# Decode attention with a gated MLP on one core: another order of TensorE's last thirty microseconds, and the last block of wo in three transfers

## The chip, the cores and the metric

The kernel runs on one core of a Trainium2 chip. The metric is the device time of one execution in microseconds (us), lower is better. Beside the time of each execution the profiler gives a span, from the first to the last instruction; the time of the same execution is some 1.9 us more. Engines are named as in the profile: PE (TensorE) multiplies matrices, DVE (VectorE) and ACT (ScalarE) work on rows, POOL (GpSimd) only prepares constants here, and SP (SyncE) issues nearly all loads, strictly in the order of its program. All engines work side by side and wait for each other by semaphores.

## The reference, cut to what matters

```python
# x [4,1,640], k_cache and v_cache [4,32,8192,192], wq [640,6144], wo [6144,640], all bf16
W = 2048                                             # max(256, 8192 // 4): the last 2048 positions
xn = _layernorm(x)
q = (xn @ wq).reshape(4, 1, 32, 192).transpose(0, 2, 1, 3)
k, v = k_cache[:, :, -W:, :], v_cache[:, :, -W:, :]
p = softmax(einsum("bhqd,bhkd->bhqk", q, k) * 192 ** -0.5)
o = einsum("bhqk,bhkd->bhqd", p, v)
attn = o.transpose(0, 2, 1, 3).reshape(4, 1, 6144) @ wo
mlp = (silu(xn @ w1) * (xn @ w3)) @ w2
out = x + attn + mlp
```

There are 4 batches, 32 heads of 192, one query each, and 32 heads of keys and values. Each head's window of K is 3 MB over the four batches, and so is its window of V; together with the weights 223 MB are read.

## The kernel before, in words

The 128 partitions hold 32 groups of positions for each of the 4 batches, so one head's K or V is one tile of 128 partitions by 64 positions by 192. There are two tiles for K (`kt`) and two for V (`vt`), used by even and odd heads in turn. The setup (layernorm, q, the MLP) lies at the start of the kernel and is not touched. Below, K31 is head 31's K, V29 is head 29's V, and so on.

For each head h:

- DVE multiplies K by q in two halves (`mult(h, 0)` and `mult(h, 1)`, L272 to L277) into the two halves of `prs`.
- PE adds up six parts of each product by an identity matrix into `ps` (`adder(0)` and `adder(1)`, L420 to L427, matmuls at L373), and DVE sums the rest into the scores `sc` (`reduce_half`, L279).
- The maximum: DVE takes each partition's maximum (`chain_lmax`, L286), PE turns it into a row (`tr`, L431), DVE takes each batch's maximum from that row (`chain_gmax`, L290), ACT scales it (`gneg`, L352), PE hands it back to all partitions (`bc`, L435), ACT copies it (`negm`, L354) and takes the exponential with its row sums (L356).
- DVE spreads the exponential over the batches (`chain_z`, L295), and PE multiplies by V (`pv`, L448) into `o_ps`, which has a single buffer.
- ACT copies `o_ps` to `o_sb` (L359), and PE gathers it for a pair of heads into `po` (`osum`, L456). `tot` (L440) gathers the pair's row sums; DVE takes the reciprocal (`norm_rec`, L299), scales `po` (`norm_og`, L304) and, at every second pair, transposes four heads' o into `oT` (L307).

PE's order is written out by hand. Heads 1 to 29's steps run in a loop of 14 turns; the last two heads and the products with wo stand behind it (L491 to L531). `proj(g)` multiplies four heads' o, group g, by their block of wo: six columns of two matmuls each, 12 matmuls, all adding into `acc` (L385). Wo 0 to 4 are loaded early into the MLP's weight tiles; wo 5 to 7 at the very end into `kt[0]`, when head 30 no longer needs it. An operation waits only for its own semaphores, but on each engine everything behind it waits with it.

Before the change, PE's order from head 30 on is, with the semaphores that each waits for left out: K30's two halves around the maximum of head 29 and o of head 28; `tot`; wo 0; V29; K31's first half; the transpose of head 30's lmax; o of head 29; bc of head 30; K31's second half; V30; wo 1; the transpose of head 31's lmax; wo 2; bc of head 31; o of head 30; wo 3 and 4; `tot`; V31 in two halves; o of head 31; wo 5, 6, 7.

The ends of the loads on SP, in order: K30, K31, V29, V30, V31's first half, V31's second half, wo 5, wo 6, wo 7's first five columns, wo 7's last column. `load_v(h)` waits until the products with V of head h - 2 are done (`s_pv`, L164), because they share a tile; for head 31 this wait stands ahead of its first half only. Wo 5 waits for a count of `s_red`, which head 30's scores bring. Loads behind a waiting load on SP are not issued either.

On ACT, each head's copy of `o_ps` (L358, L359) stands behind its exponential and ahead of the next head's `gneg`. On DVE, the odd heads' `norm_rec` waits for `s_pv` so that the pair's row sums are complete; `s_tot` is raised only by the last `tot`.

At the end DVE copies `acc` to `res` (L335), and SP and ACT each send half of it out (L201, L361).

Of the kernel before, what the change touches and what calls it, by code (L numbers as in the profile page):

```python
# [16 lines left out]
def kernel(  # L17
# [15 lines left out]
    B, Sq, D = A_x.shape  # L33
    _, H, Sk, Dh = A_k_cache.shape
# [16 lines left out]
    RPP = QW // P  # L51
# [19 lines left out]
    def sb(name, shape, dt):  # L71
        return ctx.enter_context(nc.sbuf_tensor(name, shape, dt))

    def psum(name, shape, dt):
        return ctx.enter_context(nc.psum_tensor(name, shape, dt))
# [31 lines left out]
    o_sb = [sb(f"o_sb{i}", [P, 2 * Dh], FP32) for i in range(2)]  # L107
# [6 lines left out]
    o_ps = psum("o_ps", [P, QC], FP32)  # L114
# [4 lines left out]
    def sem(name):  # L119
        return ctx.enter_context(nc.semaphore(name))  # L120

    first = sem("s_first")
    (s_x, s_wq0, s_wq1, s_wq2, s_w1, s_w3, s_w2, s_k0, s_k1, s_v31, s_wom, s_wo5, s_wo6, s_wo7a, s_wo7b,
     s_gp, s_dv, s_ac, s_pp, s_ps, s_red, s_tr, s_gmax, s_bc, s_negm, s_exp, s_pv, s_sum, s_rec, s_og, s_oT,
     s_tot, s_acc) = [sem(n) for n in (
        "s_x", "s_wq0", "s_wq1", "s_wq2", "s_w1", "s_w3", "s_w2", "s_k0", "s_k1", "s_v31", "s_wom", "s_wo5",
        "s_wo6", "s_wo7a", "s_wo7b", "s_gp", "s_dv", "s_ac", "s_pp", "s_ps", "s_red", "s_tr", "s_gmax", "s_bc",
        "s_negm", "s_exp", "s_pv", "s_sum", "s_rec", "s_og", "s_oT", "s_tot", "s_acc")]
    last = sem("s_last")
    s_pr, s_lmax, s_gneg, s_z, s_v0, s_v1, s_osb, s_fin, s_out0, s_out1 = [sem(n) for n in (  # L130
        "s_pr", "s_lmax", "s_gneg", "s_z", "s_v0", "s_v1", "s_osb", "s_fin", "s_out0", "s_out1")]
# [3 lines left out]
    def take(e, s, n=1):  # L135
        e.wait_ge(s, n).then_inc(s, -n)  # L136
# [8 lines left out]
    def wo_of(hg):  # L145
        t = wts[hg // 2][:, :] if hg < 5 else wo_end
        i = hg % 2 if hg < 5 else hg - 5
        return t[:, i * RPP * D:(i + 1) * RPP * D]

    def wo_src(hg):  # L150
        return A_wo[hg * QW:(hg + 1) * QW, :].rearrange("(p i) n -> p (i n)", i=RPP)


    sp = nc.sync
# [25 lines left out]
    for h in range(H - 2):  # L180
# [3 lines left out]
        if h in (4, 6, 8):  # L184
            g = h - 4
# [3 lines left out]
                         in_=A_wo[g * QW:(g + n) * QW, :].rearrange("(g p i) n -> p g (i n)", g=n, i=RPP)).then_inc(s_wom, 16)  # L189
# [4 lines left out]
    sp.wait_ge(s_red, 2 * (H - 2) + 1)  # L194
    for hg, s in ((5, s_wo5), (6, s_wo6)):
        sp.dma_start(out=wo_of(hg), in_=wo_src(hg)).then_inc(s, 16)
    WC = RPP - 1
    sp.dma_start(out=wo_of(7)[:, 0:WC * D], in_=wo_src(7)[:, 0:WC * D]).then_inc(s_wo7a, 16)
    sp.dma_start(out=wo_of(7)[:, WC * D:], in_=wo_src(7)[:, WC * D:]).then_inc(s_wo7b, 16)
    sp.wait_ge(s_fin, 1)  # L200
    sp.dma_start(out=out_v[:, 0:N0], in_=res[0:B, :]).then_inc(s_out0, 16)  # L201
    take(sp, s_fin)
# [25 lines left out]
    ve = nc.vector  # L228
# [43 lines left out]
    def mult(h, a):  # L272
        if a == 0:
            ve.wait_ge(s_k[h % 2], 16 * (h // 2 + 1))
        ve.tensor_tensor(out=prs[:, a].rearrange("p q j d -> p (q j) d"), in0=kt[h % 2][:, 2 * a * JQ:2 * (a + 1) * JQ, :],  # L275
                         in1=qbc[:, h * Dh:(h + 1) * Dh].unsqueeze(1).to_broadcast([P, 2 * JQ, Dh]),
                         op=ALU.mult).then_inc(s_pr, 1)  # L277

    def reduce_half(h, a):  # L279
        ve.wait_ge(s_ps, 2 * h + a + 1)  # L280
        ve.tensor_reduce(out=sc[h % 3][:, 2 * a * JQ:2 * (a + 1) * JQ], in_=ps[:, a].rearrange("p q (j d) -> p (q j) d", d=DD),  # L281
                         axis=AX.X, op=ALU.add).then_inc(s_red, 1)

    def chain_lmax(h):
        ve.wait_ge(s_red, 2 * (h + 1))
        ve.tensor_reduce(out=lmax[h % 2][:], in_=sc[h % 3][:], axis=AX.X, op=ALU.max).then_inc(s_lmax, 1)  # L286

    def chain_gmax(h):
        ve.wait_ge(s_tr, h + 1)
        ve.tensor_reduce(out=gmax[h % 2][:], in_=mt[0:1, 0:P].rearrange("o (p b) -> o b p", b=B), axis=AX.X,  # L290
                         op=ALU.max).then_inc(s_gmax, 1)
# [6 lines left out]
    def norm_rec():  # L298
        ve.reciprocal(out=rt[:], in_=mt[:, P + 1:P + 2]).then_inc(s_rec, 1)  # L299

    def norm_og(i):
        sl = slice(i % 2 * 2 * CT, (i % 2 + 1) * 2 * CT)
        ve.wait_ge(s_sum, 2 * i + 2)
        ve.tensor_scalar_mul(out=og[sl].rearrange("p i r -> p (i r)"), in0=po[sl, 0:Dh], scalar1=rt[sl, 0:1]).then_inc(s_og, 1)  # L304
        if i % 2:
            ve.wait_ge(s_og, i + 1)
            ve.transpose(out=oT[:, i // 2].rearrange("p i r -> p (i r)"), in_=flat(og)).then_inc(s_oT, 1)  # L307

    for h in range(H):
        odd = h % 2 and h > 1  # L310
        mult(h, 0)
        if h:
            reduce_half(h - 1, 1)
            if odd:
                ve.wait_ge(s_pv, h - 1)
                norm_rec()
            chain_lmax(h - 1)
        mult(h, 1)
        if h:
            chain_gmax(h - 1)  # L320
        reduce_half(h, 0)
        if odd:
            norm_og(h // 2 - 1)
        if h:
            chain_z(h - 1)
# [1 line left out]
    chain_lmax(H - 1)  # L327
    chain_gmax(H - 1)
    chain_z(H - 1)
    ve.wait_ge(s_tot, 1)  # L330
    norm_rec()
    ve.wait_ge(s_rec, NP)
    norm_og(NP - 1)
# [4 lines left out]
    ae = nc.scalar  # L338
# [8 lines left out]
            ae.copy(out=qbc[:, (c0 + i) * QC:(c0 + i + 1) * QC], in_=q_banks[i]).then_inc(s_ac, 1)  # L347
    ae.wait_ge(s_pp, 14)
    ae.activation(out=sT[:], in_=po[:, 0:FW], func=ACTF.Silu).then_inc(s_ac, 1)
    for h in range(H):  # L350
        ae.wait_ge(s_gmax, h + 1)
        ae.mul(out=gneg[h % 2][:], in_=gmax[h % 2][:].unsqueeze(1).to_broadcast([1, PB, B]), mul=-SCALE).then_inc(s_gneg, 1)  # L352
        ae.wait_ge(s_bc, h + 1)
        ae.copy(out=negm[h % 2][:], in_=mt[:, P:P + 1]).then_inc(s_negm, 1)  # L354
        ae.wait_ge(s_negm, h + 1)
        ae.activation(out=ex[h % 2][:], in_=sc[h % 3][:], func=ACTF.Exp, bias=negm[h % 2][:, 0:1], scale=SCALE,  # L356
                      accum_out=rsum[h % 2][:]).then_inc(s_exp, 1)
        ae.wait_ge(s_pv, h + 1)  # L358
        ae.copy(out=o_sb[h % 2][:], in_=o_ps[:, 0:2 * Dh]).then_inc(s_osb, 1)  # L359
    ae.wait_ge(s_fin, 1)  # L360
    ae.dma_start(out=out_v[:, N0:D], in_=res[CT:CT + B, :]).then_inc(s_out1, 16)  # L361
    take(ae, s_fin)
# [7 lines left out]
    pe = nc.tensor  # L370
# [8 lines left out]
    for kc in range(KC):  # L379
        m = pe.transpose(out=xnT_ps[:, kc, :], in_=xn[:, kc:D:KC], identity=idb[0:B, 0:B])  # L380
# [10 lines left out]
    for c0 in (0, 6):  # L391
# [3 lines left out]
        for kc in range(KC):  # L395
# [4 lines left out]
            for i, qp in enumerate(q_banks):  # L400
                m = held(qp, w, wq_rows[kc][:, (c0 + i) * QC:(c0 + i + 1) * QC], kc == 0, kc == KC - 1)
# [3 lines left out]
    for t, bank, s in ((wts[0], po, s_w1), (wts[1], mt, s_w3)):  # L405
# [3 lines left out]
        for kc in range(KC):  # L409
            for w in range(HG):  # L410
                m = pe.matmul(bank[w * CT:(w + 1) * CT, 0:FW], lhsT=xnT[:, kc].rearrange("p a b -> p (a b)")[:, 0:CT],
                              rhs=t[:, kc * F + w * FW:kc * F + (w + 1) * FW], start=(kc == 0), stop=(kc == KC - 1))
# [3 lines left out]
    for c in range(FC):  # L416
        m = acc_add(hT[:, c, 0:B], wts[2][:, c * D:(c + 1) * D])
# [11 lines left out]
    def tr(par):  # L429
        take(pe, s_lmax)  # L430
        pe.transpose(out=mt[0:1, 0:P], in_=lmax[par][:], identity=idf[:]).then_inc(s_tr, 1)  # L431
# [6 lines left out]
    def tot():  # L438
        for par in range(2):
            m = pe.matmul(mt[:, P + 1:P + 2], lhsT=flat(tot_w[:, par]), rhs=rsum[par][:], start=(par == 0), stop=(par == 1))  # L440
        return m

    def pv(par, j0=0, j1=NJ):
        if j0 == 0:
            take(pe, s_v[par], 16)
        for jj in range(j0 // 2, j1 // 2):
            c = jj % 4
            m = pe.matmul(o_ps[c * CT:c * CT + 2 * B, 0:2 * Dh].rearrange("p (a d) -> p a d", a=2), lhsT=z[par][:, 2 * jj:2 * jj + 2, :],  # L448
                          rhs=vt[par][:, 2 * jj:2 * jj + 2, :], start=(jj < 4), stop=(jj >= NJ // 2 - 4))
        if j1 == NJ:  # L450
            m.then_inc(s_pv, 1)

    def osum(par):
        take(pe, s_osb)
        for k in range(2):
            m = pe.matmul(po[:, 0:Dh], lhsT=flat(sel_w[:, par, k]),  # L456
                          rhs=o_sb[par][:, k * Dh:(k + 1) * Dh].rearrange("p (r i) -> p i r", i=RPP), start=(par + k == 0), stop=(par + k == 2))
        m.then_inc(s_sum, 1)

    def proj(hg, i0=0, i1=RPP):  # L460
        w = wo_of(hg)
        for i in range(i0, i1):
            m = acc_add(oT[:, hg, i, 0:B], w[:, i * D:(i + 1) * D], stop=(hg == NG - 1 and i == RPP - 1))
        return m
# [29 lines left out]
    bc(1)  # L494
    adder(1)
    take(pe, s_z)
    tot()
    pe.wait_ge(s_wom, 48)
    pe.wait_ge(s_oT, 5)
    proj(0)  # L500
    pv(1)
    adder(0)
    tr(0)
    osum(1)
    bc(0)
    adder(1)
    take(pe, s_z)
    pv(0)
    proj(1)
    tr(1)  # L510
    proj(2)
    bc(1)
    osum(0)
    proj(3)
    proj(4)
    take(pe, s_z)
    tot().then_inc(s_tot, 1)
    pv(1, 0, NJ // 2)
# [6 lines left out]
    pe.wait_ge(s_wo6, 16)  # L525
    proj(6)
    pe.wait_ge(s_oT, 8)
    pe.wait_ge(s_wo7a, 16)
    proj(7, 0, WC)
    pe.wait_ge(s_wo7b, 16)  # L530
    proj(7, WC, RPP).then_inc(s_acc, 1)  # L531


# [28 lines left out]
```

## Time and profile before

| What | Value |
|---|---|
| median of 3 runs | 526.82 us (526.68 to 527.18) |
| profiled execution, its own time | 526.78 us |
| its span | 524.9 us |
| mean granted TensorE clock | 0.857 |
| busy: PE, DVE, ACT, POOL | 366.4, 334.6, 54.1, 3.4 us |
| read from HBM | 222.96 MB |
| one K load, 3072 KB, median from issue to landing | 19.6 us |
| V31's halves, 1536 KB each, median from issue to landing | 10.8 us |
| out to HBM, issued at | 522.33 us of the span |

The busy times overlap, and a share of busy time does not say which engine sets the end. A line of the timeline gives the start and the length of a merged group of instructions, the engine, the line, the operation with what it writes and reads, and the number of instructions; in brackets stands the idle time just before and what ended it. Time to landing runs from the issue to the moment at which the data's semaphore has come, so it holds the time that a transfer queues behind those issued before it.

### The profile page before, as it was taken

What the parts mean: (1) busy time and instruction counts of PE and PEld (TensorE: products, weight loads), DVE (VectorE), ACT (ScalarE), POOL (GpSimd) and SP (SyncE); (2) the same over time, 40 slices, a digit from 0 to 9 for tenths busy, and PEclk for the clock granted to TensorE, in tenths of its full rate; (3) what the DMA queues carried; (4) which work ended last, traced back from release to release, by engine and by line L of the source; (5) the groups of instructions that cost most, each with busy time, mean ns of one, the idle gap of its engine ahead of it and who ended that gap; (6) DMA issues with size and microseconds to landing.
All of it is one profiled execution on the core that took longest, in us unless ns stands there. A gap on an engine that the chain in (4) does not pass through costs nothing. (4 is left out here: it accounts for less than half of the span.)

```text
span 524.9 us, 4774 instructions
## 1 busy us (share of the span) xinstructions
PE 366.4 (70%) x2306; PEld 83.7 (16%) x1553; DVE 334.6 (64%) x287; ACT 54.1 (10%) x174; POOL 3.4 (1%) x16
## 2 busy tenths in 40 slices
PE   2775777667586367876667666887676767587897
PEld 0010111111211011121111111111111112111133
DVE  3136777767267564678767676667776666666871
ACT  2120101101101011011101111110110011111010
POOL 2000000000000000000000000000000000000000
PEclk9887888878869788788878888888797888888799
DMA  8999999999999999999999999999999999999995
GB/s 356 423 441 429 428 436 426 442 421 427 443 429 436 427 427 444 429 431 438 425 440 425 438 429 433 434 429 438 425 442 423 440 429 431 438 425 440 425 424 231
DMA packets 11520, 223.07 MB, mean 425 GB/s; under 512 B 1260, under 2 KB 1400, under 8 KB 2424
## 3 DMA queue, kind: packets, MB, share of 16 engines
q1 hardware_dynamic: 11496, 222.96, 98.9%
q8 instruction: 4, 0.07, 0.0%
q14 instruction: 4, 0.03, 0.0%
q10 hardware_dynamic: 16, 0.01, 0.0%
HBM read 222.96 MB, written 0.01 MB: 425 GB/s over the span
## 5 line engine op out<-in xcount | busy, mean ns | idle before, releaser
L373 PE MATMUL ps<-prs,idb 128*128 128x512 bf16 x768 | 229.0, 461 | 134.1 <-PEq L136 134.1
L275 DVE TENSOR_TENSOR prs<-kt,qbc 128x6144 bf16<-128x6144 bf16 x64 | 214.5, 3353 | 120.1 <-DMA kt<-in_A_k_cache_dram 120.1
L281 DVE TENSOR_REDUCE sc<-ps 128x32 f32<-128x1024 f32 x64 | 77.5, 1211 | 3.3 <-PE ps L373 3.1
L456 PE MATMUL po<-o_sb,sel_w 128*128 128x192 f32 x128 | 49.0, 516 | 0.7 <-PEq L136 0.7
L448 PE MATMUL o_ps<-vt,z 128*8 128x384 bf16 x1024 | 47.2, 326 | 0.1
L352 ACT ACTIVATE gneg<-gmax 1x128 f32<-1x128 f32 x32 | 9.8, 308 | 290.1 <-DVE gmax L290 290.1
L448 PEld LDWEIGHTS o_ps<-vt,z 128*8 128x8 bf16 x1024 | 22.1, 86 | 54.6 <-issue 42.0
L422 PEld LDWEIGHTS <-idb 128*128 128x128 bf16 x64 | 6.3, 98 | 153.1 <-issue 152.6
L456 PEld LDWEIGHTS po<-o_sb,sel_w 128*128 128x128 f32 x128 | 25.3, 221 | 14.7 <-issue 5.2
L359 ACT COPY o_sb<-o_ps 128x384 f32<-128x384 f32 x32 | 15.3, 479 | 117.4 <-PE o_ps L448 117.4
L295 DVE TENSOR_TENSOR z<-ex,mask_b 128x256 bf16<-128x256 bf16 x32 | 13.6, 424 | 18.9 <-ACT ex L356 18.4
L431 PEld LDWEIGHTS mt<-idf,lmax 128*1 128x1 f32 x32 | 3.3, 104 | 118.9 <-issue 118.9
L290 DVE TENSOR_REDUCE gmax<-mt 1x4 f32<-1x128 f32 x32 | 8.8, 276 | 10.6 <-PE mt L431 10.1
L440 PEld LDWEIGHTS mt<-rsum,tot_w 128*128 128x128 f32 x64 | 9.6, 191 | 35.1 <-issue 34.7
L234 DVE CAST qbc<-ps 128x512 bf16<-128x512 f32 x4 | 2.6, 686 | 19.7 <-PE ps L373 19.7
L435 PE MATMUL mt<-one,gneg 1*128 1x1 f32 x64 | 11.9, 253 | 4.0 <-PEq L136 3.8
L373 PE MATMUL ps<-vt,xnT 128*128 128x512 bf16 x31 | 10.6, 477 | 5.0 <-DMA vt<-in_A_wq_dram 3.9
L435 PEld LDWEIGHTS mt<-one,gneg 1*128 1x128 f32 x64 | 9.4, 182 | 22.4 <-issue 22.4
L356 ACT ACTIVATE ex<-sc,negm 128x64 bf16<-128x64 f32 x32 | 11.1, 348 | 1.0
L431 PE MATMUL mt<-idf,lmax 128*1 128x128 f32 x32 | 10.5, 328 | 0.0
L304 DVE TENSOR_SCALAR og<-po,rt 64x192 bf16<-64x192 f32 x16 | 6.6, 414 | 3.8 <-PE po L456 3.6
L440 PE MATMUL mt<-rsum,tot_w 128*128 128x1 f32 x64 | 8.1, 231 | 0.0
(65 smaller groups left out, 79.6 us busy)
## 6 DMA issues: line engine op xcount, KB each, us to landing
kt<-in_A_k_cache_dram SPq DMA_DIRECT2D x32, 3072.0 KB, 19.6
vt<-in_A_v_cache_dram SPq DMA_DIRECT2D x31, 3072.0 KB, 22.5
vt<-in_A_wq_dram SPq DMA_DIRECT2D x2, 3072.0 KB, 13.2
wt<-in_B_w_dram SPq DMA_DIRECT2D x3, 1920.0 KB, 27.8
wt<-in_A_wo_dram SPq DMA_DIRECT2D x2, 1920.0 KB, 28.6
vt<-in_A_v_cache_dram SPq DMA_DIRECT2D x2, 1536.0 KB, 10.8
kt<-in_A_wo_dram SPq DMA_DIRECT2D x2, 960.0 KB, 14.6
prs<-in_A_wq_dram SPq DMA_DIRECT2D x1, 1536.0 KB, 19.9
```

The costliest lines, as they stand in the source:

```text
L275: ve.tensor_tensor(out=prs[:, a].rearrange("p q j d -> p (q j) d"), in0=kt[h % 2][:, 2 * a * JQ:2 * (a + 1) * JQ, :], in1=qbc[:, h * Dh:(h ...
L281: ve.tensor_reduce(out=sc[h % 3][:, 2 * a * JQ:2 * (a + 1) * JQ], in_=ps[:, a].rearrange("p q (j d) -> p (q j) d", d=DD), axis=AX.X, op=AL ...
L295: ve.tensor_tensor(out=z[h % 2][:], in0=ex[h % 2][:].unsqueeze(2).to_broadcast([P, NJ, B]), in1=mask_b[:].unsqueeze(1).to_broadcast([P, NJ ...
L352: ae.mul(out=gneg[h % 2][:], in_=gmax[h % 2][:].unsqueeze(1).to_broadcast([1, PB, B]), mul=-SCALE).then_inc(s_gneg, 1)
L356: ae.activation(out=ex[h % 2][:], in_=sc[h % 3][:], func=ACTF.Exp, bias=negm[h % 2][:, 0:1], scale=SCALE, accum_out=rsum[h % 2][:]).then_i ...
L359: ae.copy(out=o_sb[h % 2][:], in_=o_ps[:, 0:2 * Dh]).then_inc(s_osb, 1)
L373: return pe.add_instruction(mybir.InstMatmult(name=nc.get_next_instruction_name(), engine=pe.engine, ins=[pe.lower_ap(rhs), pe.lower_ap(lh ...
L431: pe.transpose(out=mt[0:1, 0:P], in_=lmax[par][:], identity=idf[:]).then_inc(s_tr, 1)
L435: pe.matmul(mt[:, P:P + 1], lhsT=flat(gneg[par]), rhs=one[:], start=True, stop=True).then_inc(s_bc, 1)
L440: m = pe.matmul(mt[:, P + 1:P + 2], lhsT=flat(tot_w[:, par]), rhs=rsum[par][:], start=(par == 0), stop=(par == 1))
L448: m = pe.matmul(o_ps[c * CT:c * CT + 2 * B, 0:2 * Dh].rearrange("p (a d) -> p a d", a=2), lhsT=z[par][:, 2 * jj:2 * jj + 2, :], rhs=vt[par ...
L456: m = pe.matmul(po[:, 0:Dh], lhsT=flat(sel_w[:, par, k]), rhs=o_sb[par][:, k * Dh:(k + 1) * Dh].rearrange("p (r i) -> p i r", i=RPP), star ...
```

## The change

On TensorE, behind the loop: wo 0 to 4 stand together behind the first `tot`; then come K31's first half and the transpose of head 30's lmax, and only then V29, o of head 29, bc, and K31's second half. The transpose of head 31's lmax stands ahead of V30. `tot` of heads 28 and 29 raises `s_tot` as well.

On DVE, head 31's `norm_rec` waits for the first count of `s_tot` in place of `s_pv`, and the last one for the second count.

On ACT, the copies of heads 30's and 31's `o_ps` stand behind the loop over the heads, so that head 30's comes behind head 31's exponential; head 29's stays where it was.

On SP, wo 7 is loaded as three, two and one columns in three transfers, where it was five and one; TensorE waits for each.

```diff
-    WC = RPP - 1
-    sp.dma_start(out=wo_of(7)[:, 0:WC * D], in_=wo_src(7)[:, 0:WC * D]).then_inc(s_wo7a, 16)
-    sp.dma_start(out=wo_of(7)[:, WC * D:], in_=wo_src(7)[:, WC * D:]).then_inc(s_wo7b, 16)
+    last_cols = ((0, 3, s_wo7a), (3, 5, s_wo7b), (5, RPP, s_wo7c))
+    for i0, i1, s in last_cols:
+        sp.dma_start(out=wo_of(7)[:, i0 * D:i1 * D], in_=wo_src(7)[:, i0 * D:i1 * D]).then_inc(s, 16)
...
             if odd:
-                ve.wait_ge(s_pv, h - 1)
+                if h < H - 1:
+                    ve.wait_ge(s_pv, h - 1)
+                else:
+                    ve.wait_ge(s_tot, 1)
                 norm_rec()
...
-    ve.wait_ge(s_tot, 1)
+    ve.wait_ge(s_tot, 2)
     norm_rec()
...
+    def o_copy(h):
+        ae.wait_ge(s_pv, h + 1)
+        ae.copy(out=o_sb[h % 2][:], in_=o_ps[:, 0:2 * Dh]).then_inc(s_osb, 1)
+
...
-        ae.wait_ge(s_pv, h + 1)
-        ae.copy(out=o_sb[h % 2][:], in_=o_ps[:, 0:2 * Dh]).then_inc(s_osb, 1)
+        if h < H - 2:
+            o_copy(h)
+    o_copy(H - 2)
+    o_copy(H - 1)
...
     take(pe, s_z)
-    tot()
+    tot().then_inc(s_tot, 1)
     pe.wait_ge(s_wom, 48)
     pe.wait_ge(s_oT, 5)
-    proj(0)
-    pv(1)
+    for g in range(5):
+        proj(g)
     adder(0)
     tr(0)
+    pv(1)
     osum(1)
     bc(0)
     adder(1)
     take(pe, s_z)
+    tr(1)
     pv(0)
-    proj(1)
-    tr(1)
-    proj(2)
     bc(1)
     osum(0)
-    proj(3)
-    proj(4)
     take(pe, s_z)
     tot().then_inc(s_tot, 1)
...
-    pe.wait_ge(s_wo7a, 16)
-    proj(7, 0, WC)
-    pe.wait_ge(s_wo7b, 16)
-    proj(7, WC, RPP).then_inc(s_acc, 1)
+    for i0, i1, s in last_cols:
+        pe.wait_ge(s, 16)
+        m = proj(7, i0, i1)
+    m.then_inc(s_acc, 1)
```

More of the change, by code (lines that the diff above doesn't have):

```diff
@@ L122 @@
     first = sem("s_first")
-    (s_x, s_wq0, s_wq1, s_wq2, s_w1, s_w3, s_w2, s_k0, s_k1, s_v31, s_wom, s_wo5, s_wo6, s_wo7a, s_wo7b,
+    (s_x, s_wq0, s_wq1, s_wq2, s_w1, s_w3, s_w2, s_k0, s_k1, s_v31, s_wom, s_wo5, s_wo6, s_wo7a, s_wo7b, s_wo7c,
      s_gp, s_dv, s_ac, s_pp, s_ps, s_red, s_tr, s_gmax, s_bc, s_negm, s_exp, s_pv, s_sum, s_rec, s_og, s_oT,
@@ L126 @@
         "s_x", "s_wq0", "s_wq1", "s_wq2", "s_w1", "s_w3", "s_w2", "s_k0", "s_k1", "s_v31", "s_wom", "s_wo5",
-        "s_wo6", "s_wo7a", "s_wo7b", "s_gp", "s_dv", "s_ac", "s_pp", "s_ps", "s_red", "s_tr", "s_gmax", "s_bc",
+        "s_wo6", "s_wo7a", "s_wo7b", "s_wo7c", "s_gp", "s_dv", "s_ac", "s_pp", "s_ps", "s_red", "s_tr", "s_gmax", "s_bc",
         "s_negm", "s_exp", "s_pv", "s_sum", "s_rec", "s_og", "s_oT", "s_tot", "s_acc")]
```

## The prediction

> **What bounds the kernel now.** I read the page first: is any engine full?
>
> ```profile
> DMA  8999999999999999999999999999999999999995
> ...
> HBM read 222.96 MB, written 0.01 MB: 425 GB/s over the span
> ```
>
> The DMA engines are, in 39 of 40 slices; no compute engine passes 70% of the span. So the time is the stream of loads plus what follows its end, and the change touches only the last 30 us. The chain of waits ends there:
>
> ```profile
> 517.59 1.58 PE po L456 x4
> 519.17 2.56 PE acc L385 x36
> ...
> 521.82 0.48 DVE res L335
> ```
>
> The end is TensorE work, o of head 31 (L456) and then the products of wo 5, 6 and 7 without a gap, and not a wait for wo 7. From the last product at 521.73 to the span's end at 524.93 it is 3.2 us. Now the timeline of those 30 us, start and length in us:
>
> ```profile
> 496.33 3.35 DVE L275 TENSOR_TENSOR prs<-kt,qbc 128x6144 bf16<-128x6144 bf16 x1
> ...
> 498.26 0.98 PE L385 MATMUL acc<-wt,oT 128*4 128x320 bf16 x12
> ...
> 499.29 1.47 PE L448 MATMUL o_ps<-vt,z 128*8 128x384 bf16 x32
> ...
> 500.69 2.76 PE L373 MATMUL ps<-prs,idb 128*128 128x512 bf16 x12
> ...
> 503.30 0.27 PE L431 MATMUL mt<-idf,lmax 128*1 128x128 f32 x1
> ...
> 503.40 1.52 PE L456 MATMUL po<-o_sb,sel_w 128*128 128x192 f32 x4
> ...
> 505.32 2.76 PE L373 MATMUL ps<-prs,idb 128*128 128x512 bf16 x12
> ...
> 508.12 1.23 DVE L281 TENSOR_REDUCE sc<-ps 128x32 f32<-128x1024 f32 x1 [1.61 <-PE ps L373]
> ...
> 509.38 0.22 DVE L286 TENSOR_REDUCE lmax<-sc 128x1 f32<-128x64 f32 x1
> ...
> 513.18 1.79 PE L385 MATMUL acc<-wt,oT 128*4 128x320 bf16 x24
> ...
> 515.44 1.47 PE L448 MATMUL o_ps<-vt,z 128*8 128x384 bf16 x32
> ...
> 516.97 0.48 ACT L359 COPY o_sb<-o_ps 128x384 f32<-128x384 f32 x1 [4.59 <-PE o_ps L448]
> ```
>
> The first line is K31's first product on VectorE. It carries no wait: K31, issued at 479.44 and 12.4 us in flight, was there at 491.8, and VectorE came to it in order. TensorE reaches wo 0 at 498.26; the product ends at 499.68. So TensorE does not wait for K31: from wo 0 to the end it is filled, by V29 (499.29), K31's first half (500.69), K31's second half (505.32), V30, wo 1 and so on. Last, the transfers' issues and their time to landing:
>
> ```profile
> 500.80 0.54 SPq L167 DMA_DIRECT2D vt<-in_A_v_cache_dram  x1
> vt<-in_A_v_cache_dram SPq DMA_DIRECT2D x1, 3072.0 KB, 22.7
> kt<-in_A_wo_dram SPq DMA_DIRECT2D x1, 800.0 KB, 16.9
> kt<-in_A_wo_dram SPq DMA_DIRECT2D x1, 160.0 KB, 16.0
> ```
>
> The first is V31's first half, issued 0.04 us after V29's products end at 500.76, because load_v waits for them. The second is V30: issued at 483.76, landed at 506.46. So the queue had 5.7 us in hand when V31 was issued. Wo 7's two parts, issued at 503.44 and 504.64, landed at 520.34 and 520.64. TensorE ended at 521.73, some 1.1 us behind the stream: the most that a better order could win, less the last column's own work.
>
> **The change, part by part,** as steps from the start of one TensorE group to the next (from the timeline), beginning at wo 0 at 498.26, which does not move. Before, from there to the last product: 23.47 us.
>
> 1. Wo 0 to 4 in a row. Twenty-four of these matmuls step 1.72 us (513.18 to the next group at 514.90), so five blocks of 12 take 5 × 0.86 = 4.30; with the turn to the next group 4.35. K31's first half starts at 502.6, not 500.69; its product has been ready since 499.68, so the wait there was worth 1.4 us at the most, and 4.35 us of work is put into it.
> 2. K31's first half, 2.61 to the transpose of lmax of head 30 (500.69 to 503.30). That lmax no longer needs V29 (it waits for s_tot) and is done near 501.1, so no wait. The transpose steps 0.20 (510.22 to 510.42).
> 3. V29 now starts at about 505.4 instead of 499.29. o of head 29 is next and needs ScalarE's copy of V29's result; before, K31's first half stood between and hid that copy. The pair without cover is the one at the end: 515.44 to 517.59, 2.15. O itself steps 1.53 (511.64 to 513.17), bc 0.30.
> 4. K31's second half, and right behind it the transpose of head 31's lmax, which was covered by V30 and wo 1. The bare path is 2.80 (505.32 to 508.12), 1.26 for the reduction, 0.22 for lmax, and 0.2 for wake and weights: 4.48, where the matmuls alone take 2.76. This wait of 1.7 us is new; queued behind it are V30, bc, o and V31, everything to the end. Transpose 0.20, V30 1.35 (between 1.30 and 1.40 in the two rows above).
> 5. bc, then o of head 30. Its copy by ScalarE now stands behind head 31's negm and exponential. From bc's start: negm at 0.40, exponential at 0.59, the copy after its accumulator read at 1.05, copied at 1.53, o at 1.67. Before, o followed bc by 0.31. O steps 1.53.
> 6. tot 0.54, V31 2.15, o of head 31 1.51, wo 5 to 7 2.63: as before. Wo 3 and 4, 1.72 us, no longer stand ahead of tot.
>
> Sum: 4.35 + 2.61 + 0.20 + 2.15 + 1.53 + 0.30 + 4.48 + 0.20 + 1.35 + 1.67 + 1.53 + 0.54 + 2.15 + 1.51 + 2.63 = **27.20, or 3.7 us more** than 23.47. The work is the same; what comes in is three naked waits (0.6 + 1.7 + 1.3). Steps not shown before in this order are the wakes in 3, 4 and 5: at nothing (0.5 less), and with blocks of 0.82, the sum is 26.5 (+3.0); with 1.0 a block (498.26 to V29's 499.29, +0.65) and 0.2 more for each of the three wakes it is 28.4 (+4.9). A gain is excluded, since no work goes away. I take the middle rows.
>
> **The loads.** V31's first half is issued when V29 ends, at about 506.9 + 0.04: 0.5 us *after* V30 has landed, and SP holds V31's second half and all of wo 5 to 7 behind it. The queue runs dry. For a dry queue the nearest row is the kernel's start: issued at 0.96, first packets near 2.0, and in the first 20 us 7.51 MB, which at 425 GB/s is 17.7 us: full rate as from 2.3, 1.35 after issue. Before, the last load landed 14.2 us after V30. Restarted at 508.3 it lands at about 522.5, 1.9 us later; at no restart cost 521.1, at twice it 523.9. On TensorE, wo 5 starts at 498.26 + 24.57 = 522.8 and wo 7 at 524.6: the loads stay hidden, with some 2.5 us in hand. The split of wo 7 costs an issue of 0.43 on SP, which is 15 us ahead, and one more landing: 160 KB came 0.3 behind the 800 KB part, so 0 to 0.3, hidden too. Its gain is hidden as well, since TensorE comes after the data.
>
> The Trainium skill, in "DMA: Bandwidth & Descriptors" (Latency and other measured facts), puts a HWDGE transfer's first byte at about 0.6 us. The row above shows about 1.0. By the page the loads would land some 0.4 us earlier, still behind TensorE, and the time would be the same.
>
> So the last product ends at 525.5, the span at 524.9 + 3.7 = 528.6, and the profiled time of 526.78 (1.9 around the span; 0.04 under the median of 526.82) becomes **530.5 us**, +0.7%.
>
> **Rivals.**
> A. *The loads set the end, and TensorE keeps up with them* (chance 0.08). For it: V31 is issued late in any case. Last landing 522.5, 0.3 for one column, 3.2 to the span's end, 1.9 around it: 527.9 to 528. Against it: TensorE would have to lose 2.5 us less than summed.
> B. *Faster* (0.03): wo 0 to 4 fit into a wait for K31, V29 ends before V30 has landed, and the end falls onto wo 7's last column: 520.64 + 0.3 + 3.2 + 1.9 = 526.0. It decides if V31's issue stays ahead of about 505 (V30's landing less the restart), that is if V29 starts by 503.5. Against it: K31 landed at 491.8, and the rows put V29 at 505.4.
> C. *No change* (0.03): the waits cost about what the shorter tail saves: 526.3 to 527.3.
> D. *TensorE's clock falls* (0.05). In the stretch from 488.15 to 493.40, behind 4.4 us without a matmul, the granted clock was 0.50, and K31's counterpart, K30's first half, took 5.28 instead of 2.76. One such stretch on the new path costs 2 to 3 us: 532.5 to 533.5. Against: from 493.75 to 521.7 the clock was 1.00, and the longest gap I expect is 1.8 us. The Trainium skill, "TensorE: Matmul & The Clock Gate" (Part 1: The HAM clock gate), asks for an idle window of about 3.4 us before the clock halves; by it the clock stays whole and D adds nothing.
>
> **How the numbers follow.** The forecast has 0.81, with its own range of 529.8 to 531.7 from the two sums. Reaching a little towards A, 529.2 to 531.9 holds about 8 in 10. Faster and slower mean by over 0.2% (1.05 us), about what a measurement of this kernel tells from no change. Slower: forecast, A and D, 0.94; same 0.03; faster 0.03.
>
> **What would show it.** Right: V31's first half issued near 507 and a hole in the DMA row behind V30's landing; a gap of about 1.7 us on TensorE after K31's second half, ended by lmax; o of head 30 starting 1.5 us or more after bc; the last 36 products still without a gap, ending near 525.5. Wrong: V31 issued before 505, TensorE waiting for K31 rather than for lmax, or a wait for wo 7 just ahead of the last two products.

## The result, and the profile after

The changed kernel takes **530.55 us** (median of 4, 530.14 to 530.83) against 527.0 (median of 4) on the same chip: ratio 1.0064, 95% interval 1.0047 to 1.008. It is slower by 3.5 us, and the forecast was 530.5. The profiled execution takes 530.51 us, with a span of 528.7. The size is right; how it comes about is only partly what the prediction said, and the chain of waits shows that at once (start, length, what):

```profile
504.83 1.43 PE o_ps L457 x32
...
506.28 0.54 SPq L167
...
509.38 15.30 DMA kt<-in_A_wo_dram
...
524.73 0.71 PE acc L394 x6
...
525.53 0.48 DVE res L338
```

Before, the end was TensorE's own work. Now it goes back from wo 7's products to a load, from there to SP, where the load's issue stood behind V31's, and from V31's issue to V29's products. The timeline of the changed kernel shows both halves of the story:

```profile
497.79 4.24 PE L394 MATMUL acc<-wt,oT 128*4 128x320 bf16 x60
...
501.96 2.76 PE L382 MATMUL ps<-prs,idb 128*128 128x512 bf16 x12
...
504.76 1.47 PE L457 MATMUL o_ps<-vt,z 128*8 128x384 bf16 x32
...
506.28 1.18 SPq L167 DMA_DIRECT2D vt<-in_A_v_cache_dram  x2
...
506.91 1.58 PE L465 MATMUL po<-o_sb,sel_w 128*128 128x192 f32 x4 [0.68 <-PEq L136]
...
508.73 2.76 PE L382 MATMUL ps<-prs,idb 128*128 128x512 bf16 x12
...
512.79 0.22 DVE L286 TENSOR_REDUCE lmax<-sc 128x1 f32<-128x64 f32 x1
...
513.15 0.27 PE L440 MATMUL mt<-idf,lmax 128*1 128x128 f32 x1 [1.66 <-PEq L136]
...
516.31 1.58 PE L465 MATMUL po<-o_sb,sel_w 128*128 128x192 f32 x4 [1.18 <-PEq L136]
...
521.82 1.98 PE L394 MATMUL acc<-kt,oT 128*4 128x320 bf16 x24
...
525.12 0.08 PEld L394 LDWEIGHTS acc<-kt,oT 128*4 128x4 bf16 x2 [0.30 <-DMA kt<-in_A_wo_dram]
```

Line 1 is wo 0 to 4 in a row. V29's products start at 504.76 (499.29 before), V31 is issued at 506.28 (500.80 before). The three naked waits stand in brackets: 0.68 for ACT's copy of head 29, 1.66 for head 31's lmax, 1.18 for the copy of head 30. TensorE reaches wo 5 at 521.82; from there it took 2.63 before, which would be 524.4. But the last column's weights wait for their data until 525.12, and the products end at 525.44: the loads are 1.0 us behind TensorE. The stretches of one microsecond show why (stretch, length, busy time of PE, PEld, DVE, ACT and POOL with counts, clock, share of the DMA engines, GB/s):

```profile
503.00:504.00 1.00, 1.00 (x6) 0.00 (x0) 0.87 (x1) 0.00 (x0) 0.00 (x0) 1.00 1.14 492
504.00:505.00 1.00, 1.00 (x13) 0.26 (x13) 0.13 (x1) 0.00 (x0) 0.00 (x0) 1.00 0.29 123
505.00:506.00 1.00, 1.00 (x32) 0.51 (x24) 1.00 (x2) 0.00 (x0) 0.00 (x0) 1.00 0.12 49
506.00:507.00 1.00, 0.33 (x9) 0.12 (x2) 0.28 (x1) 0.68 (x2) 0.00 (x0) 1.00 0.00 0
507.00:508.00 1.00, 1.00 (x4) 0.59 (x4) 0.00 (x0) 0.00 (x0) 0.00 (x0) 1.00 0.45 98
508.00:509.00 1.00, 1.00 (x6) 0.39 (x3) 0.41 (x1) 0.16 (x1) 0.00 (x0) 1.00 1.01 356
509.00:510.00 1.00, 1.00 (x6) 0.00 (x0) 0.42 (x1) 0.44 (x2) 0.00 (x0) 1.00 0.92 332
510.00:511.00 1.00, 1.00 (x6) 0.00 (x0) 0.00 (x0) 0.00 (x0) 0.00 (x0) 1.00 0.82 295
```

V30 counts as landed at 506.96, when the last DMA engine is done with it, but the stream is nearly gone from 504 on: the share of the DMA engines falls to 0.29, 0.12 and nothing. V31, issued at 506.28, brings data from 507.6, and then the rate stays at 295 to 356 GB/s for some four microseconds. So two things happened, and each alone may be the whole loss: TensorE's waits and the late loads. The experiments had to take them apart.

### The profile page after: what moved, and what is told of

It reads as the page before. It is cut to its first block, busy times and chain, and to the rows that moved or that the text cites. A ratio compares the mean times of both kernels' runs of the same rounds, so it can differ in the third digit from the quotient of the medians.

```text
span 528.7 us, 4775 instructions
## 1 busy us (share of the span) xinstructions
PE 363.1 (69%) x2306; PEld 82.9 (16%) x1553; DVE 334.3 (63%) x287; ACT 53.9 (10%) x174; POOL 3.4 (1%) x16
## 5 line engine op out<-in xcount | busy, mean ns | idle before, releaser
L465 PEld LDWEIGHTS po<-o_sb,sel_w 128*128 128x128 f32 x128 | 25.2, 220 | 15.9 <-issue 6.3
L290 DVE TENSOR_REDUCE gmax<-mt 1x4 f32<-1x128 f32 x32 | 8.9, 277 | 11.3 <-PE mt L440 11.2
L361 ACT COPY negm<-mt 128x1 f32<-128x1 f32 x32 | 5.1, 159 | 31.4 <-PE mt L444 31.4
```

The costliest lines, as they stand in the source:

```text
L465: m = pe.matmul(po[:, 0:Dh], lhsT=flat(sel_w[:, par, k]), rhs=o_sb[par][:, k * Dh:(k + 1) * Dh].rearrange("p (r i) -> p i r", i=RPP), star ...
```

## The experiments

Each variant was timed beside the kernel before, whose medians were 526.96 to 527.01 us. A profile is of one execution, which can be faster or slower than the median, and the time is not always 1.9 us over the span: in one execution of a variant it was 528.12 us with a span of 524.6.

**Wo 7 in three transfers alone**, on the kernel before:

```diff
-    sp.dma_start(out=wo_of(7)[:, 0:WC * D], in_=wo_src(7)[:, 0:WC * D]).then_inc(s_wo7a, 16)
-    sp.dma_start(out=wo_of(7)[:, WC * D:], in_=wo_src(7)[:, WC * D:]).then_inc(s_wo7b, 16)
+    for i0, i1, s in last_cols:
+        sp.dma_start(out=wo_of(7)[:, i0 * D:i1 * D], in_=wo_src(7)[:, i0 * D:i1 * D]).then_inc(s, 16)
```

> The kernel before with only wo 7 split into three, two and one columns. The changed kernel's trace suggests two costs side by side (theory): TensorE's new order alone would end the last product 2.7 us later than before, and V31's late issue ends the loads 4.4 us later, so that the loads come out on top by about 1.0 us. Rival 1: TensorE's naked waits alone make the time. Rival 2: the late loads alone make it. All three expect nothing of the split here, since in the kernel before TensorE ends behind the loads: 526.8 to 527.3. If one more transfer costs more than the 0.3 us by which wo 7's last column landed behind the part ahead of it, the time is over 527.5.

Measured: 527.34 us, ratio 1.0005 (0.9996 to 1.0014). No difference, as expected (the median is 0.04 over the expected range); the chain still ends with TensorE's 36 products without a wait.

**V31 late alone**, with TensorE's order as before:

```diff
+    sp.wait_ge(s_exp, H - 1)
     load_v(H - 1, 0, NJ // 2)
```

> The kernel before with only one wait added on SP: V31's first half is not issued before head 30's exponential is done (506.1 us in the trace of before, where V30 lands at 506.46), as late against V30's landing as in the changed kernel. TensorE's order is as before. Theory, and rival 2: from issue to the last column of wo 7 it took 18.8 us in the changed kernel, so the last column lands at 524.9 and the time is 529.9 to 530.4. With the restart of 1.35 us that the prediction took, the last landing is at 521.7 and the time 527.1. Rival 1: the loads stay hidden, 526.8 to 527.0.

Measured: 530.96 us, ratio 1.0078 (1.0065 to 1.0091). V31's late issue alone costs 4.0 us, more than the whole change. V31 was issued at 506.31, 0.4 us ahead of V30's landing, and the last column landed at 525.12, 18.4 us behind V30. The end of the time has a second cause, though; TensorE's timeline and its stretches in this run:

```profile
515.67 0.82 PE L449 MATMUL o_ps<-vt,z 128*8 128x384 bf16 x16
518.26 0.95 PE L449 MATMUL o_ps<-vt,z 128*8 128x384 bf16 x16 [1.77 <-DMA vt<-in_A_v_cache_dram]
519.88 1.68 PE L457 MATMUL po<-o_sb,sel_w 128*128 128x192 f32 x4 [0.66 <-PEq L136]
521.50 4.70 PE L386 MATMUL acc<-kt,oT 128*4 128x320 bf16 x36
```

```profile
515.41:518.82 3.41, 1.64 (x35) 0.84 (x35) 0.17 (x1) 0.00 (x0) 0.00 (x0) 1.00 0.97 403
518.82:522.23 3.41, 2.75 (x18) 1.48 (x12) 0.52 (x2) 0.48 (x1) 0.00 (x0) 0.50 1.02 429
```

TensorE waited 1.77 us for V31's second half, the clock fell to 0.50, and the last 36 products took 4.70 instead of 2.61. They end at 526.2, about 0.8 behind what the loads alone would give (525.12 + 0.3). So some 3.2 of the 4.0 us are the loads', by this one profile, and the rest is the falling clock's.

**TensorE's order alone**: the changed kernel, with V31 in K30's tile, so that it needn't wait for V29, and wo 5 to 7 in V29's:

```diff
-    wo_end = flat(kt[0])
+    wo_end = flat(vt[1])
...
-            if h >= 2:
+            if h == H - 1:
+                sp.wait_ge(s_red, 2 * (H - 2) + 1)
+            elif h >= 2:
...
+        t = kt[0] if h == H - 1 else vt[h % 2]
...
-    sp.wait_ge(s_red, 2 * (H - 2) + 1)
+    sp.wait_ge(s_pv, H - 2)
...
-    pv(1, 0, NJ // 2)
+    pv(1, 0, NJ // 2, kt[0])
     pe.wait_ge(s_v31, 16)
-    pv(1, NJ // 2, NJ)
+    pv(1, NJ // 2, NJ, kt[0])
```

> The changed kernel with V31 loaded into the tile that held K30, so that it no longer waits for V29's products, and wo 5 to 7 into V29's tile in exchange. The queue does not run dry; TensorE's order is that of the change. Theory: TensorE's waits remain and set the end at 524.4 us by the changed kernel's steps, 1.0 us earlier than measured there: 529.3 to 529.7. Rival 1: no difference, 530.5. Rival 2: the whole loss goes, 526.0 to 527.0.

Measured: 530.86 us, ratio 1.0073 (1.006 to 1.0086). No difference from the changed kernel, as rival 1 had it, though V31 was issued at 495.26 and the stream had no hole. The profiled execution took 530.14 us, the shortest of its five. The chain of waits and the first step:

```profile
498.41 4.24 PE L397 MATMUL acc<-wt,oT 128*4 128x320 bf16 x60
```

```profile
520.93 1.58 PE po L472 x4
522.51 2.56 PE acc L397 x36
```

No wait for a load is left, and from wo 0 to the last product (525.07) it is 26.66 us: the prediction's steps gave 27.20. So the order alone costs the whole loss, and the reading by which only the loads did it is out. In the changed kernel the same stretch, with the loads on top, is 27.65; the 1.0 us between them doesn't show in the time. In the two profiled executions 0.6 of it went away ahead of wo 0, which started at 498.41 here and at 497.79 there, since K30's first half took 5.28 us at a low clock here and 4.44 there. Whether that holds for the other executions stays open.

**Wo 1 to 4 back into the waits**, the rest of the change kept:

```diff
-    for g in range(5):
-        proj(g)
+    proj(0)
     adder(0)
     tr(0)
     pv(1)
+    proj(4)
     osum(1)
     bc(0)
     adder(1)
     take(pe, s_z)
+    proj(1)
+    proj(2)
     tr(1)
     pv(0)
     bc(1)
+    proj(3)
     osum(0)
```

> The changed kernel with wo 1 to 4 taken out from ahead of K31's first half and put into the waits that the new order has: wo 4 behind V29, wo 1 and 2 behind K31's second half, wo 3 behind bc of head 31. All else is as changed. V29 should start near 502.0 and V31 be issued near 503.5, 2.4 us ahead of V30's landing, so that the queue does not run dry. Theory: the waits are filled, the last product ends near 522.2 by the steps, 527.5 to 528.0. Rival 1: the same number from TensorE alone. Rival 2, or a price for late issue that sets in before the queue is empty: the loads end behind 522, and the time is over 528.

Measured: 527.80 us, ratio 1.0017 (1.0008 to 1.0026): most of the loss goes, and the number is the theory's. Its end is not: the last products wait for wo 7 (landed at 522.21), though V31 was issued 3.5 us ahead of V30's landing.

**Wo 0 to 4 in a row alone**, on the kernel before:

```diff
-    proj(0)
+    for g in range(5):
+        proj(g)
     pv(1)
...
-    proj(1)
     tr(1)
-    proj(2)
...
-    proj(3)
-    proj(4)
```

> The kernel before with only wo 0 to 4 in a row where wo 0 stood; V29 stays ahead of K31's first half, and all the rest is as before. V29 then starts near 502.6 and V31 is issued near 504.2, some 2.3 us ahead of V30's landing. By the steps TensorE ends at 522.7 (527.8 us). If late issue costs the loads before the queue is empty, as the low rate behind V31's issue in the run with wo put back suggests, the last landing is near 523 and the time 528.2 to 528.8. If only an empty queue costs, 527.5 to 528.0. If the whole loss came from K31's half and the two maxima being moved, there is none here: 526.8 to 527.2.

Measured: 528.88 us, ratio 1.0039 (1.0027 to 1.0052), just over the expected. V31 was issued at 502.91, 3.9 us ahead of V30's landing, and again the last products wait 1.04 us for wo 7. This and the run above suggested that a load may be late long before the queue is empty.

**A lead of 3 us alone**, TensorE's order as before:

```diff
+    sp.wait_ge(s_ps, 2 * (H - 1) + 1)
     load_v(H - 1, 0, NJ // 2)
```

> The kernel before with one wait added on SP: V31 is not issued before K31's first half is added up (503.45 us in the trace of before), some 3.0 us ahead of V30's landing; before it was 5.7. TensorE's order is as before. If a late issue costs before the queue is empty (the last column landed 14.2 us behind V30 at a lead of 5.7, 15.5 at 3.5 to 3.9, 18.1 and 18.4 at 0.7 and 0.4), the last column lands some 16 us behind V30, at 522.5, and the time is 527.8 to 528.4. If only an empty queue costs, as the prediction had it (restart 1.35 us), it is 526.8 to 527.2.

Measured: 528.69 us, ratio 1.0032 (1.0021 to 1.0042), a little over the expected. Its stretches behind the issue at 503.59:

```profile
503.00:504.00 1.00, 1.00 (x6) 0.56 (x4) 1.00 (x1) 0.00 (x0) 0.00 (x0) 1.00 1.06 442
504.00:505.00 1.00, 1.00 (x4) 0.24 (x2) 1.00 (x3) 0.31 (x1) 0.00 (x0) 1.00 0.31 111
505.00:506.00 1.00, 0.89 (x6) 0.39 (x3) 1.00 (x2) 0.45 (x3) 0.00 (x0) 1.00 1.04 295
506.00:507.00 1.00, 1.00 (x7) 0.00 (x0) 0.53 (x2) 0.15 (x2) 0.00 (x0) 1.00 0.96 344
507.00:508.00 1.00, 1.00 (x6) 0.00 (x0) 0.00 (x0) 0.00 (x0) 0.00 (x0) 1.00 0.97 356
```

The kernel before in two of these stretches:

```profile
504.00:505.00 1.00, 0.92 (x3) 0.21 (x1) 1.00 (x3) 0.31 (x1) 0.00 (x0) 1.00 0.84 344
505.00:506.00 1.00, 0.96 (x6) 0.39 (x3) 1.00 (x2) 0.55 (x3) 0.00 (x0) 1.00 1.01 430
```

The hole is there although V30 landed only at 506.58. From the issues and times to landing (known to 0.1 us) of the profiled executions, in order of lead:

| Kernel | V31 issued | V30 landed | lead | GB/s from 504 to 506 | last landing behind V30 |
|---|---|---|---|---|---|
| wo in the wait for K30, V31 in K30's tile (below) | 494.36 | 506.81 | 12.4 | 379 | 15.1 |
| wo split, V31 in K30's tile (below) | 494.37 | 506.69 | 12.3 | 385 | 14.2 |
| TensorE's order alone | 495.26 | 506.59 | 11.3 | 381 | 14.3 |
| wo 0 to 4 in the wait for K30 (below) | 500.85 | 506.60 | 5.8 | 369 | 14.2 |
| wo 7 in three alone | 501.00 | 506.75 | 5.8 | 344 | 14.2 |
| before | 500.80 | 506.46 | 5.7 | 387 | 14.2 |
| wo split (below) | 501.68 | 506.52 | 4.8 | 387 | 14.3 |
| wo in the wait for K30, wo 7 in three (below) | 502.73 | 507.03 | 4.3 | 326 | 16.0 |
| wo in a row alone | 502.91 | 506.79 | 3.9 | 270 | 15.6 |
| wo back in the waits | 503.21 | 506.69 | 3.5 | 260 | 15.5 |
| lead of 3 us | 503.59 | 506.58 | 3.0 | 203 | 15.9 |
| changed | 506.28 | 506.96 | 0.7 | 86 | 18.1 |
| V31 late | 506.31 | 506.68 | 0.4 | 74 | 18.4 |

Below a lead of 4.8 us the rate from 504 to 506 falls step by step with the lead. In time, 4.8 and more cost nothing that shows here, with one exception, 3.0 to 4.3 cost 1.3 to 1.8, and 0.4 to 0.7 cost about 4. The exception is the first row: with a lead of 12.4 us and no hole its last load came 0.9 later all the same, after a rate of 332 and 307 GB/s from 507 to 509. Its cause isn't known. So a difference of 1 us in the last column isn't always the lead's, and each row is one execution.

**Wo 0 to 4 where TensorE really waits**, ahead of K30's first half; the rest as before. Then the same with wo 7 in three, and with V31 in K30's tile besides:

```diff
         pe.reg_add(cnt, cnt, 1)
 
+    pe.wait_ge(s_wom, 48)
+    pe.wait_ge(s_oT, 5)
+    for g in range(5):
+        proj(g)
     adder(0)
...
-    pe.wait_ge(s_wom, 48)
-    pe.wait_ge(s_oT, 5)
-    proj(0)
     pv(1)
...
-    proj(1)
     tr(1)
-    proj(2)
...
-    proj(3)
-    proj(4)
```

> The kernel before with only wo 0 to 4 moved further up: behind the loop and ahead of K30's first half, where TensorE has nothing to do for 4.4 us (483.7 to 488.15 in the trace of before) until K30 has come. Their 4.3 us just fit. The order behind is as before without wo. V31 is issued when it was or earlier. TensorE should end behind the loads, then: wo 7's five columns land at 520.3, ten products 0.7, the last column 0.2: 521.3, 0.4 us earlier than before: 526.3 to 526.7. If TensorE's order is not what matters at the end, there is no difference, 526.8 to 527.2; if the five blocks don't fit into the wait, K30's first half is late and the time is over 527.2.

> As the run with wo 0 to 4 in the wait for K30, and wo 7 in three transfers besides, so that only the last column's two products are left when the last data land: products end at about 520.9, 525.8 to 526.3. If the split costs more in the stream than it saves at the end: as without it, or longer.

> As the run with wo 0 to 4 in the wait for K30 and wo 7 in three, and V31 loaded into K30's tile, wo 5 to 7 into V29's, so that V31 is issued at about 495 instead of 500.8, with a full queue ahead of it. In the trace of before the rate falls to 385 and 344 GB/s for two microseconds behind V31's issue. If that dip comes from issuing late, some 0.2 us are won against the run without this: 525.6 to 526.1; if not, the same.

Measured: 527.30 (1.0005, 0.9996 to 1.0014), 527.54 (1.0012, 1.0002 to 1.0021) and 527.24 us (1.0003, 0.9994 to 1.0012). The expected gains are missing in all three medians. The profiled execution of the first took 526.52 us, inside the range expected; its others went up to 528.58, and no profile shows why. In the profiled one, TensorE's timeline reads

```profile
499.33 1.47 PE L448 MATMUL o_ps<-vt,z 128*8 128x384 bf16 x32 [2.45 <-PEq L136]
...
520.47 0.98 PE L385 MATMUL acc<-kt,oT 128*4 128x320 bf16 x12 [1.05 <-DMA kt<-in_A_wo_dram]
```

The end lies with the loads, as meant (products until 521.46, before 521.73). But V29 lands at 499.2, and without wo 0 TensorE is idle for 2.45 us ahead of it. In the second run, such a gap was followed by a low clock:

```profile
497.40:499.90 2.50, 0.04 (x1) 0.00 (x0) 2.50 (x2) 0.00 (x0) 0.00 (x0) 0.93 0.96 413
499.90:502.70 2.80, 2.75 (x33) 1.07 (x33) 0.04 (x1) 0.00 (x0) 0.00 (x0) 0.50 1.06 456
```

V29's products took 2.73 instead of 1.47, and V31 was issued at 502.73, 4.3 us ahead of V30's landing; the last load landed 16.0 behind V30. The third has a lead of 12.4 us, but its clock fell twice, and TensorE set the end again (products until 522.40).

**Split between the two gaps**: wo 0 to 2 ahead of K30, wo 3 and 4 ahead of V29, wo 7 in three; then with V31 in K30's tile:

```diff
+    pe.wait_ge(s_wom, 48)
+    pe.wait_ge(s_oT, 5)
+    for g in range(3):
+        proj(g)
     adder(0)
...
-    pe.wait_ge(s_wom, 48)
-    pe.wait_ge(s_oT, 5)
-    proj(0)
+    proj(3)
+    proj(4)
     pv(1)
...
-    proj(1)
     tr(1)
-    proj(2)
...
-    proj(3)
-    proj(4)
```

> The kernel before with wo 0 to 2 in the wait for K30, wo 3 and 4 ahead of V29 (where the run with all five in the wait for K30 left TensorE idle for 2.4 us, and in one execution let its clock fall), and wo 7 in three transfers. No new wait, V31 issued near 500.8, TensorE behind the loads at the end: last column at 520.7, products at 521.0: 525.9 to 526.5. If the end moves with the stream of loads and not with TensorE: 526.8 to 527.4.

> As the run with wo 0 to 2 in the wait for K30 and wo 3 and 4 ahead of V29, with V31 loaded into K30's tile and wo 5 to 7 into V29's, so that V31 has a lead of over 11 us. If a lead of 5.7 us still costs some, 0.1 to 0.3 us less than the run without; otherwise the same.

Measured: 526.71 us, ratio 0.9992 (0.9982 to 1.0002), and **526.31 us, ratio 0.9989 (0.998 to 0.9998)**. The first lies between its two expected ranges. The second is the fastest of all, 0.7 us under the kernel before, and its interval just leaves out no change; of eleven variants, one such interval is weak evidence, and that of wo ahead of K30 with wo 7 in three leaves it out by as little on the other side. The second's chain of waits ends on wo 7's second transfer, with the six products of the second and third behind it:

```profile
503.47 17.09 DMA vt<-in_A_wo_dram
...
520.60 0.72 PE acc L388 x6
```

The two differ by 0.4 us, and their intervals overlap: that V31's longer lead did it isn't shown.

## Why the prediction was right, and where it was not

- **TensorE doesn't wait for K31, so wo 0 to 4 push K31, V29 and V31 back: right.** K31's first half went from 500.69 to 501.96, V29 from 499.29 to 504.76.
- **Three naked waits: right**, at 0.68, 1.66 and 1.18 us, where 0.6, 1.7 and 1.3 were summed. The sum of steps of 27.20 was 0.54 too high: 26.66 where the loads were kept away. Of that, 0.18 is in wo 0 to 4 (4.17 for 4.35) and 0.34 in the steps from head 31's bc to V31 (3.40 for 3.74).
- **"The loads stay hidden, with some 2.5 us in hand": wrong.** This is the step that failed, and the term is the 14.2 us from V30's landing to the last one, added to a restart of 1.35 us. The last load landed 4.4 us later, not 1.9. V31 was even issued 0.7 us ahead of V30's landing, where 0.5 behind it was forecast, and the restart was near its size: first data 1.3 us after the issue. But V30's landing is that of the slowest DMA engine. In the kernel before V31's first data came at 504.1, 2.3 us ahead of V30's landing, and from there to the last landing it took 16.5 us, not 14.2; in the changed kernel it took 17.5 from 507.6, since the stream came back slowly. The bound named for the faster rival, an issue ahead of about 505, is wrong for the same reason: 502.9 to 503.6 already cost 1.3 to 1.7 us.
- **The sign of a wrong prediction appeared**: a wait for wo 7 ahead of the last two products (0.30). Rival A's mechanism, with a chance of 0.08, did set the end, though at the forecast's price. The forecast of 525.5 for the last product met 525.44 because wo 0 started 0.47 earlier and the steps were 0.54 shorter, while the loads added 1.0. That these cancel to 0.1 us is luck; that the time is near 530.5 is not, since TensorE's order alone gives 530.86.
- **Rival D**, the falling clock: not in the changed kernel (1.00 from wo 0 on), but in five variants.
- **The split of wo 7 costs nothing: right** by the run of it alone.
- **A reading of the page:** the row of the DMA engines shows 90% or more in 38 of the 40 slices, not 39. Nothing in the sum hangs on it.

The Trainium skill, "DMA: Bandwidth & Descriptors" (Latency and other measured facts), gives about 0.6 us to a HWDGE transfer's first byte. In the changed kernel it was 1.3 us (506.28 to 507.6). The slow return behind it cost about 1 us more, an estimate from the rates between 508 and 512: 323 GB/s, where the kernel before moved 415 in the same microseconds.

## What to carry to other kernels

Before work is moved into a wait, look at which wait it is: here TensorE's idle time lay ahead of K30 (4.4 us) and, some, ahead of V29, and the place chosen had almost none (0.6 us in the run with wo 1 to 4 put back). A load that waits for a consumer should be measured by its issue's lead over the landing ahead of it; where the lead shrinks, as it did here from 5.7 to 0.7 us, look at the stream's rate in the microseconds ahead of that landing, since most of the DMA engines may be done by then (here their share was 0.29 and 0.12). When two chains of waits end within a microsecond of each other, one sum that fits the time doesn't prove its mechanism: take each chain away once.

## What the runs showed of the hardware that was not expected

The clock of TensorE fell behind gaps much shorter than 3.4 us. The Trainium skill, "TensorE: Matmul & The Clock Gate" (Part 1: The HAM clock gate), has the clock halve after an idle window of that length. In every profile here a stretch of one clock, but for the last, lasts a multiple of 3.41 us. In the run with V31 late, a stretch of 3.41 us with 1.64 us of work was followed by 0.50, as shown above. In the run with wo split between two gaps it was less idle still:

```profile
490.90:494.31 3.41, 2.32 (x11) 1.02 (x7) 3.27 (x3) 0.67 (x3) 0.00 (x0) 1.00 0.94 404
494.31:497.72 3.41, 3.41 (x10) 0.00 (x0) 3.14 (x2) 0.24 (x2) 0.00 (x0) 0.50 1.02 440
```

The longest gap there is 1.09 us, and K30's second half then took 4.45 us, which takes 2.76 at the full clock. In the first run with wo ahead of K30 a gap of 2.45 us left the clock at 1.00, and one stretch of 3.41 us there, from 498.04, had only 2.12 us of work. So neither the longest gap nor the busy time alone decides, and what does isn't settled by these runs.
